# Issuing the output weight's four transfers from SyncE, between two chunks' loads, in a fused retention and gated-unit kernel

## The chip, the cores and the metric

The kernel runs on one core of a Trainium2 chip. A core has five engines that run side by side [...]: TensorE (matrix products, PE in the profile), VectorE (DVE), ScalarE (ACT), GpSimd (POOL) and SyncE (SP), which here does nothing but issue transfers. Each engine takes its instructions in program order, so an instruction that waits holds up all that stand behind it on the same engine. Transfers between HBM and the on-chip memory are issued by SyncE or ScalarE and carried by 16 DMA engines. The metric is the device time of one execution in microseconds (us), median over runs; lower is better.

## The reference

A retention layer (attention without softmax, with an exponential decay per head) feeds a gated linear unit whose gate is a causal convolution. In essence, with B = 8, H = 8 heads, S = 576 positions, D = 64, and a model width of 512:

```python
scores = (q @ k.transpose(0, 1, 3, 2)) / sqrt(D)
Dmat   = where(rel >= 0, gamma[h] ** rel, 0)         # rel = i - j
x      = ((scores * Dmat) @ v)                       # heads side by side: (B, S, 512)
gate   = sigmoid(sum_k conv_w[k] * x[:, s - 4 + k])  # five causal taps per channel
out    = (gate * (x @ w_val)) @ w_out
```

All inputs and the output are float32. `w_val` and `w_out` are 512 x 512 (1 MB each); q, k and v have 9.4 MB each.

## The kernel before

The sequence of each batch is cut into two "double chunks" of 256 positions and a tail of 64; the tails of four batches are gathered into one more chunk of the same size. That gives 18 chunks, numbered m = 0 to 17 here (so the fourth and the fifth are m = 3 and m = 4). The whole order of instructions is written out by hand (`manual_schedule`), so what an engine does next is read off the program text.

For each chunk the work goes through these steps.

- **Loads** (`load`, line 98, through `fetch`, line 85): k, q and v of the chunk, 512 KB each, all issued by SyncE (line 90; 95 for the gathered tails). Chunks 0 to 2 have buffers of their own; later ones share two buffers per tensor (`LB = 2`), so chunk m + 2 can be loaded only when chunk m has been cast out of its buffer. Loads up to chunk 4 are issued ahead of the loop (lines 106 to 124); the loop issues chunk m + 4 at the end of iteration m (line 595).
- **Casts** to bf16 (`cast_k`, `cast_q`, `cast_v`, lines 226 to 239), mostly on GpSimd, for chunk m + 2 in iteration m.
- **Turning** keys and queries with TensorE transposes (`turn`, line 253), copied out by ScalarE (`take_turned`, line 262, into the tile `kq`).
- **Scores** (line 277), masked by VectorE (`masks`, line 287, tile `p`), products with v (`values`, line 309), the **state** that carries earlier positions (`update`, line 356, tile `st`; copied out by ScalarE in `take_state`, line 367, as `sd` or `sl`) and its use (`carried`, line 316). VectorE takes the result as `x` (`take_x`, line 335); GpSimd copies its last four positions into the next chunk (`pass_on`, line 347).
- **The gated unit**, one or two chunks behind: the convolution as products with diagonals (`conv`, line 386, tile `dg`), the sigmoid on ScalarE (`gate`, line 401), the product with `w_val` (`value`, line 406; weights `wvb`, cast from `wvf` by `prep_wv`, line 211), and the product with `w_out` (`project`, line 416; weights `wob`), whose result ScalarE copies out (`ob`, line 428) and SyncE stores (line 430).

The loop (line 504) runs iteration m for chunk m. TensorE's order inside one iteration is: first scores, convolution of chunk m - 1, state, second scores, turning of chunk m + 1's keys, part of the gated unit, values, turning of chunk m + 1's queries, the rest of the gated unit. A "stage" below is the time from one iteration's first scores to the next one's.

`w_out` is used for the first time in iteration 3, where `prep_wo` (line 126) casts the two halves of the tile `wof` into `wob`, one on ScalarE, one on VectorE (lines 567 and 568). `wof` is loaded by `load_wo` (line 118): four transfers of 256 KB, each filling 64 partitions of two of the four column blocks, in the order of `ORDER` (line 114). They are issued by ScalarE, and `load_wo` is called in iteration 1, after that iteration's two copies of turned keys and queries (line 562). The next instruction of ScalarE is iteration 2's first `take_state`.

Of the kernel before, what the change touches and what calls it, by code (L numbers as in the profile page):

```python
# [21 lines left out]
def kernel(  # L22
# [10 lines left out]
    nc = tc.nc  # L33
# [4 lines left out]
    HP = 64  # L38
# [42 lines left out]
    with tc.manual_schedule():  # L81
# [16 lines left out]
        def load(name, m):  # L98
            t = ld.tile([P, H, R, D], F32, name=f"f{name}" + ("e" if m < 3 else ""),
                        bufs=3 if m < 3 else LB)  # L100
            fetch(nc.sync, t, {"q": q, "k": k, "v": v}[name], m)
            loaded[name, m] = t
# [12 lines left out]
        wof = consts.tile([P, NP, DM], F32, name="wof")  # L115
        wob = consts.tile([P, NP, DM], BF16, name="wob")

        def load_wo():
            src = moe_w_out.rearrange("(pr ab hl p) n -> ab hl p pr n", pr=2, ab=2, hl=2)
            for (p0, blk, ab, hl) in ORDER:  # L120
                nc.scalar.dma_start(out=wof[p0:p0 + HP, blk:blk + 2, :], in_=src[ab, hl])

        for name in "kqv":
            load(name, 4)

        def prep_wo(copy, part):
            copy(wob[:, 2 * part:2 * part + 2], wof[:, 2 * part:2 * part + 2])  # L127
# [113 lines left out]
        def run(*lists):  # L241

            for k in range(max(map(len, lists), default=0)):
                for group in lists:
                    for f in group[k] if k < len(group) else []:
                        f()
# [30 lines left out]
        def scores(m, r, spare=False):  # L277
            s = [ps_g.tile([P, NP, P], F32, name="g") if spare else ps_s.tile([P, NP, P], F32, name=f"s{i}")
                 for i in range(2)]
            sps[m, r] = s  # L280
            n = P if dcs[m][0] == "full" else TAIL
            return [[mm(s[i][half[ab], pr, 0:n], lhsT=kq[m][half[i], 0, pr, r, half[ab]],
                        rhs=kq[m][half[i], 1, pr, cols(m, r), half[ab]],
                        start=(pr == 0), stop=(pr == NP - 1))
                     for i in range(2) for ab in range(2)] for pr in range(NP)]

        def masks(m, r, i):
            p = pp.tile([P, NP, P], BF16, name=f"p{i}")
            n = P if dcs[m][0] == "full" else TAIL
            nc.vector.tensor_tensor(p[:, :, 0:n], sps[m, r][i][:, :, 0:n],  # L290
                                    mask[dcs[m][0], r].unsqueeze(1).to_broadcast([P, NP, n]), op=ALU.mult)
            pt[m, r, i] = p
# [63 lines left out]
        def update(m, ab):  # L356
            if m >= ND or dcs[m][0] != "full":
                return []
            kind, b, c = dcs[m]
            if b not in st:  # L360
                st[b] = ps_st.tile([P, NP, D], F32, name="st")
            return [[mm(st[b][half[i], pr, :], lhsT=kbf[m][half[ab], pr, r, i, :],
                        rhs=vbf[m][half[ab], head(pr, i), r, :],
                        start=(c == 0 and ab == 0 and pr == 0 and r == 0), stop=(c == NCH - 1 and ab == 1 and r == R - 1))
                     for r in range(R) for i in range(2)] for pr in range(NP)]

        def take_state(m, ab):

            if m >= ND or dcs[m][0] != "full":
                return  # L370
            kind, b, c = dcs[m]
            last = ab == 1 and c == NCH - 1
            t = tp_sb.tile([P, NP, D], BF16, name="sl" if last else "sd", bufs=GB if last else 4)
            nc.scalar.copy(t, st[b])  # L374
            before[("tail", b) if last else (m, 1) if ab == 0 else (m + 1, 0)] = t
# [10 lines left out]
        def conv(n):  # L386

            g = [ps_g.tile([P, 2, 2 * P], F32, name="g") for _ in range(2)][::-1]
            gps[n] = g
            gsb[n] = {}  # L390
            lists = [], []
            for pr in range(2):
                a, b = 2 * pr, 2 * pr + 1
                for kk in range(KC):
                    for bank, rows, blks in ((0, half[1], (a, b)), (1, half[0], (a, b))):
                        lists[bank].append([mm(g[bank][half[i], pr, :], lhsT=dg[rows, blks[i], kk, :],
                                               rhs=xs(n, rows, blks[i], kk), start=(pr == 0 and kk == 0),
                                               stop=(pr == 1 and kk == KC - 1)) for i in range(2)])
            return lists

        def gate(n, i):
            t = gp.tile([P, 2, 2 * P], F32, name=f"gate{i}")
            nc.scalar.activation(t, gps[n][i], AF.Sigmoid)  # L403
            gsb[n][i] = t
# [99 lines left out]
        for m in range(1, ND + 1):  # L504
            now, nxt, last = ok(m), ok(m + 1), m == ND
            late = m < 4
            hi, lo = conv(m - 1)

            if now and m > 1:
                run(scores(m, 0))  # L510
                masks(m, 0, 0)
                masks(m, 0, 1)
            if last:
                run(lo, hi)
                gate(m - 1, 1)
                gate(m - 1, 0)
            elif late:
                run(lo[0:8], hi[0:8])
                run(pairs(update(m, 0)), hi[8:10])
                take_state(m, 0)  # L520
                gate(m - 1, 0)
                run(pairs(update(m, 1)), lo[8:10])
                take_state(m, 1)
                gate(m - 1, 1)
                run(carried(m, 1))
            else:
                run(carried(m, 1))
                run(pairs(update(m, 1)), lo[0:2])
                take_state(m, 1)
                run(lo[2:10], hi[0:8])  # L530
                gate(m - 1, 1)
                run(pairs(update(m + 1, 0)), hi[8:10])
                take_state(m + 1, 0)
                gate(m - 1, 0)
            if now:
                run(scores(m, 1))
                masks(m, 1, 0)
                masks(m, 1, 1)

            if last:  # L540
                value(m - 1, 1, spare(ps_s, "s1"))
                value(m - 1, 0, spare(ps_s, "s0"))
                project(m - 2, 0)
                project(m - 2, 1)
                project(m - 1, 0, last=True)
                project(m - 1, 1, last=True)
                continue
            def turn_keys():
                if nxt:
                    bank = turn(0, m + 1)  # L550
                    take_turned(0, m + 1, bank)

            def turn_queries():
                if nxt:
                    bank = turn(1, m + 1, spare(ps_g, "g", [P, NP, R, P], BF16) if m == 1 else None)
                    take_turned(1, m + 1, bank)

            if m != 2:
                turn_keys()
            if m == 1:  # L560
                turn_queries()
                load_wo()

            if m == 2:
                prep_wv(s_copy, 0)
            if m == 3:
                prep_wo(s_copy, 0)
                prep_wo(v_copy, 1)
            for (f, n, i) in {1: (), 2: ((value, 0, 1), (value, 0, 0)),
                              3: ((value, 2, 1), (project, 0, 0), (project, 0, 1))}.get(  # L570
                                  m, ((value, m - 1, 1), (project, m - 2, 0))):
                f(n, i)
            if m == 2:
                turn_keys()
            if ok(m + 2):
                cast_k(m + 2)
                cast_q(m + 2)
                cast_v(m + 2)

            run(*values(m, 1))  # L580
            run(*values(m, 0))
            run(carried(m, 0))
            take_x(m, 0)
            take_x(m, 1)
            pass_on(m)

            if m > 1:
                turn_queries()
            for (f, n, i) in {1: (), 2: ((value, 1, 1), (value, 1, 0)),
                              3: ((value, 2, 0), (project, 1, 0), (project, 1, 1))}.get(  # L590
                                  m, ((value, m - 1, 0), (project, m - 2, 1))):
                f(n, i)
            for name in "kqv":
                if ok(m + 2 + LB):
                    load(name, m + 2 + LB)
            if m == 3:
                run(update(m + 1, 0))
                take_state(m + 1, 0)
# [28 lines left out]
```

## Time and profile before

| | |
|---|---|
| device time, median of three runs | 176.76 us (175.93 to 177.71) |
| span of the profiled execution | 177.2 us |
| TensorE busy (matmul) | 146.5 us, 83% |
| VectorE busy | 102.9 us, 58% |
| ScalarE busy | 92.8 us, 52% |
| GpSimd busy | 82.2 us, 46% |
| moved by DMA | 40.35 MB, mean 228 GB/s |
| mean granted TensorE clock | 0.949 |

The profile shows the span in 40 slices of 4.43 us, with a digit for the busy tenths of each engine. They tell stages with different limits apart, which the shares above average away:

```profile
PE   7658840069879999999998899999999999999870
ACT  3745610062376657576565557657565765643340
POOL 4898686400803626334764864468456344000000
PEclk9987998556999999999999999999999999999998
DMA  4999999999203695889999998999999686122134
```

Three stretches can be seen: a start in which the loads of the first chunks and the setup of masks and decay factors share the engines; a hole of TensorE and a slow recovery between 25 and 50 us; and a long, even part in which TensorE is nearly always busy and one stage takes about 7.5 us. In the lists of waits a line "A x <- B y" says that engine A, before its instruction that writes x, sat idle until engine B's instruction y ended; the numbers are the total in us, how often, and the longest. PEclk is the clock that TensorE was granted, in tenths of full speed. In timelines the columns are start, duration, engine, line and instruction, with the idle time before it in brackets. "SPq" and "ACTq" are the issue of transfers by SyncE and ScalarE.

### The profile page before, as it was taken

To read this page: it belongs to the slowest core of one execution; us is meant where nothing else is said; L and a number is where in the kernel's file an instruction comes from. 1 tells how busy PE (TensorE), PEld (TensorE's weight loads), DVE (VectorE), ACT (ScalarE), POOL (GpSimd) and SP (SyncE) were. 2 spreads that over 40 slices of the span, in tenths; PEclk is the share of its full clock that TensorE was granted. 3 is DMA by queue.
4 is the path that set the end of the run, shared out by engine and by line. 5 is a ranking of instruction groups with operands and counts; after the bars stand their busy time and mean duration, and the time that the engine had idled before them with its cause. 6 is when DMAs were issued, how large, how long until landed. Compare 5 with 4: busy or idle time off the path is not lost.

```text
span 177.2 us, 7698 instructions
## 1 busy us (share of the span) xinstructions
PE 146.5 (83%) x3348; PEld 107.4 (61%) x3381; DVE 102.9 (58%) x187; ACT 92.8 (52%) x151; POOL 82.2 (46%) x120
## 2 busy tenths in 40 slices
PE   7658840069879999999998899999999999999870
PEld 2235730057655867778676677677678776776620
DVE  6893550025654566777645576677667776766220
ACT  3745610062376657576565557657565765643340
POOL 4898686400803626334764864468456344000000
PEclk9987998556999999999999999999999999999998
DMA  4999999999203695889999998999999686122134
GB/s 141 347 347 367 353 295 283 268 233 269 78 4 118 221 292 159 187 218 292 303 340 304 313 292 256 287 276 302 286 278 289 155 185 223 64 95 82 67 118 118
DMA packets 69631, 40.35 MB, mean 228 GB/s; under 512 B 14794, under 2 KB 63966, under 8 KB 69598
## 3 DMA queue, kind: packets, MB, share of 16 engines
q1 hardware_dynamic: 68832, 38.54, 74.6%
q10 hardware_dynamic: 766, 1.32, 2.9%
q8 instruction: 26, 0.43, 1.0%
q14 instruction: 7, 0.06, 0.1%
HBM read 30.42 MB, written 9.44 MB: 225 GB/s over the span
## 4 chain that ended last, share of the span: by engine, by line
PE 70%; SPq 13%; DMA 6%; ACT 4%; issue 3%; DVE 1%; ACTq 0%
PE g L410 17%; PE g L420 16%; SPq L90 12%; PE g L249 11%; PE tps L259 10%; PE o L304 7%; PE s L249 5%; DMA fv<-in_v_dram 3%; DMA wof<-in_moe_w_out_dram 3%; PE st L249 3%; ACT kq L267 1%; PE s L410 1%; SPq L110 1%; ACT ob L428 1%; ACT sd L374 1%
## 5 line engine op out<-in xcount | busy, mean ns | idle before, releaser
L290 DVE TENSOR_TENSOR p<-s,mask 128x512 bf16<-128x512 f32 x62 | 39.9, 686 | 31.6 <-PE s L249 31.6
L267 ACT COPY kq<-tps 128x1024 bf16<-128x1024 bf16 (+2 forms) x33 | 32.6, 991 | 15.6 <-PE tps L259 15.3
L420 PE MATMUL g<-wob,z 128*128 128x512 bf16 x113 | 34.6, 379 | 2.9 <-ACT wob L127 1.2
L410 PE MATMUL g<-x,wvb 128*128 128x256 bf16 x272 | 36.6, 281 | 0.2 <-ACT gate L403 0.2
L428 ACT COPY ob<-g 128x512 f32<-128x512 f32 x34 | 19.9, 585 | 25.0 <-PE g L420 22.8
L237 POOL TENSOR_TENSOR vb<-fv,gin 128x1024 bf16<-128x1024 f32 x15 | 28.5, 1902 | 8.7 <-DMA fv<-in_v_dram 8.5
L249 PE MATMUL g<-x,dg 64*64 64x256 bf16 x720 | 30.7, 273 | 1.3 <-DVE x L339 0.6
L339 DVE TENSOR_TENSOR x<-o,gout 128x512 bf16<-128x512 f32 x32 | 22.1, 744 | 15.8 <-PE o L304 15.8
L410 PEld LDWEIGHTS <-wvb 128*128 128x128 bf16 x288 | 27.3, 100 | 4.0 <-issue 0.6
L413 DVE TENSOR_TENSOR z<-gate,g 128x512 bf16<-128x512 f32 x34 | 23.4, 687 | 8.9 <-PE g L410 8.1
L403 ACT ACTIVATE gate<-g 128x512 f32<-128x512 f32 x36 | 21.3, 604 | 10.5 <-DVE p L290 5.4
L249 PEld LDWEIGHTS <-dg 64*64 64x64 bf16 x720 | 23.1, 105 | 4.1 <-issue 2.3
L249 PE MATMUL st<-vb,kb 64*64 64x64 bf16 x512 | 13.8, 195 | 13.1 <-ACT sd L374 12.9
L352 POOL COPY x<-x 128x16 bf16<-128x16 bf16 x16 | 3.1, 196 | 45.6 <-DVE x L339 44.4
L223 POOL CAST qb<-fq 128x512 bf16<-128x512 f32 x30 | 17.6, 613 | 10.7 <-DMA fq<-in_q_dram 9.8
L420 PEld LDWEIGHTS <-z 128*128 128x128 bf16 x144 | 14.0, 98 | 11.9 <-issue 1.6
L249 PEld LDWEIGHTS <-kb 64*64 64x64 bf16 x512 | 12.3, 111 | 14.3 <-issue 14.3
L374 ACT CAST sd<-st 128x256 bf16<-128x256 f32 x24 | 8.9, 370 | 21.3 <-DMA wof<-in_moe_w_out_dram 13.6
L223 POOL CAST kb<-fk 128x512 bf16<-128x512 f32 x30 | 17.6, 613 | 5.2 <-DMA fk<-in_k_dram 3.8
L249 PE MATMUL s<-kq 64*64 64x128 bf16 (+1 forms) x560 | 16.6, 220 | 3.2 <-DVE kq L267 1.2
L249 PEld LDWEIGHTS <-kq 64*64 64x64 bf16 x576 | 11.9, 108 | 10.4 <-issue 10.4
L304 PEld LDWEIGHTS <-vb 64*64 64x64 bf16 x576 | 9.0, 112 | 7.7 <-issue 7.6
(74 smaller groups left out, 133.0 us busy)
## 6 DMA issues: line engine op xcount, KB each, us to landing
out_dram<-ob SPq DMA_DIRECT2D x32, 256.0 KB, 3.7
fk<-in_k_dram SPq DMA_DIRECT2D x26, 256.0 KB, 4.6
fq<-in_q_dram SPq DMA_DIRECT2D x26, 256.0 KB, 5.2
fv<-in_v_dram SPq DMA_DIRECT2D x26, 256.0 KB, 5.7
fke<-in_k_dram SPq DMA_DIRECT2D x3, 512.0 KB, 6.0
fqe<-in_q_dram SPq DMA_DIRECT2D x3, 512.0 KB, 5.4
fve<-in_v_dram SPq DMA_DIRECT2D x3, 512.0 KB, 6.0
wvf<-in_moe_w_val_dram SPq DMA_DIRECT2D x1, 1024.0 KB, 8.7
```

What stands on the lines that cost most here:

```text
L223: copy(dst[:, i], src[:, :, 1:3] if i else src[:, :, 0::3])
L237: eng.tensor_tensor(vbf[m][:, h:h + n], loaded["v", m][:, h:h + n], g[:, h:h + n].unsqueeze(3).to_broadcast([P, n, R, D]), op=ALU.mult)
L249: return lambda: nc.tensor.matmul(*a, skip_group_check=True, **kw)
L267: copy(kq[m][:, which, o:o + n], bank[:, o:o + n])
L290: nc.vector.tensor_tensor(p[:, :, 0:n], sps[m, r][i][:, :, 0:n], mask[dcs[m][0], r].unsqueeze(1).to_broadcast([P, NP, n]), op=ALU.mult)
L304: nc.tensor.matmul(o, start=key not in opened, stop=False, skip_group_check=True, **kw)
L339: nc.vector.tensor_tensor(xg[b // GB][c][:, b % GB, :, x0:x0 + P].rearrange("p o (n r) -> p o r n", r=R), ops[m, ab], gout[:, :, t0:t0 + P ...
L403: nc.scalar.activation(t, gps[n][i], AF.Sigmoid)
L410: nc.tensor.matmul(vps[:, j, :], lhsT=wvb[:, o, 2 * i + j, :], rhs=xs(n, slice(0, P), o, PAD), start=(j == 0 and o == 0), stop=(j == 1 and ...
L413: nc.vector.tensor_tensor(z, gsb[n][i], vps, op=ALU.mult)
L420: nc.tensor.matmul(o, lhsT=zsb[n, j // 2][:, j % 2, i * P:(i + 1) * P], rhs=wob[:, j, :], start=(j == 0), stop=(j == NP - 1))
L428: nc.scalar.copy(ob, o)
```

## The change

The four transfers of `w_out` are issued by SyncE in place of ScalarE, and earlier in the program: `load_wo` is now called right where it is defined, after the loads of chunk 3 have been issued and before those of chunk 4. Its call in iteration 1 is gone. Tiles, shapes, the casts of `w_out` and all else stay as they were. It is meant to keep ScalarE free of transfers in the middle of the computation, and to have `w_out` in the same queue as the loads, in an order chosen by hand.

```diff
@@ -118,8 +118,9 @@
         def load_wo():
             src = moe_w_out.rearrange("(pr ab hl p) n -> ab hl p pr n", pr=2, ab=2, hl=2)
             for (p0, blk, ab, hl) in ORDER:
-                nc.scalar.dma_start(out=wof[p0:p0 + HP, blk:blk + 2, :], in_=src[ab, hl])
-
+                nc.sync.dma_start(out=wof[p0:p0 + HP, blk:blk + 2, :], in_=src[ab, hl])
+
+        load_wo()
         for name in "kqv":
             load(name, 4)
 
@@ -559,7 +560,6 @@
                 turn_keys()
             if m == 1:
                 turn_queries()
-                load_wo()
 
             if m == 2:
                 prep_wv(s_copy, 0)
```

## The prediction

> **What bounds the kernel now.** I read the page's list of costliest groups first, then all waits from 18 to 60 us, then ScalarE's timeline, SyncE's and TensorE's over that stretch, then the table by stage. Over the span TensorE is the busiest engine (146.5 of 177.2 us), and from 53.9 us to the end the chain of waits runs almost wholly through it. An average says nothing of one hole, though, and the page's slices show one: TensorE has two slices at 0 (each 4.43 us, from 26.6 us). The waits of that stretch name who is missing:
>
> ```profile
> POOL x L352 <- DVE x L339: 18.7, 2, 11.8
> DVE p L290 <- PE s L249: 18.2, 5, 13.2
> PEld L249 <- issue: 14.7, 7, 11.7
> ACT sd L374 <- DMA wof<-in_moe_w_out_dram: 13.6, 1, 13.6
> PE st L249 <- ACT sd L374: 12.5, 3, 11.6
> ```
>
> Columns: total us, times, longest. Four engines have one wait of 11.6 to 13.6 us each, and they form a chain: GpSimd's copy waits for VectorE's x, VectorE for TensorE's scores, TensorE for ScalarE's copy of the state (sd, line 374), ScalarE for "wof". ScalarE's own timeline shows what that is:
>
> ```profile
> 21.89 1.02 ACT L267 COPY kq<-g 128x1024 bf16<-128x1024 bf16 x1
> 28.94 7.50 ACTq L121 DMA_DIRECT2D wof<-in_moe_w_out_dram  x4
> 36.48 0.37 ACT L374 CAST sd<-st 128x256 bf16<-128x256 f32 x1 [13.57 <-DMA wof<-in_moe_w_out_dram]
> 36.75 0.60 ACT L403 ACTIVATE gate<-g 128x512 f32<-128x512 f32 x1
> ```
>
> Columns: start, duration, instruction, idle before. ScalarE ends a copy at 22.91, the next four instructions in its order are the w_out issues, the first starts at 28.94, the fourth ends at about 36.4, and the sd copy starts at once. That copy does not read w_out; it stands behind the issues. TensorE has been done with its input since 25.27 us:
>
> ```profile
> 25.01 0.26 PE L249 MATMUL st<-vb,kb 64*64 64x64 bf16 x6
> 36.90 0.26 PE L249 MATMUL st<-vb,kb 64*64 64x64 bf16 x3 [11.61 <-ACT sd L374]
> ...
> 38.14 3.59 PE L410 MATMUL g<-x,wvb 128*128 128x256 bf16 x16
> 41.53 1.06 PE L259 MATMUL tps<-ident,kb 128*128 128x128 bf16 x8
> ```
>
> Why do four issues last so long? SyncE's timeline is a row of loads without a pause, and the DMA share is full; the tables (core, stretch, busy times, then PEclk, DMA share, GB/s):
>
> ```profile
> 22.96:25.30 2.34, 1.75 (x68) 1.45 (x68) 2.12 (x4) 0.00 (x0) 1.73 (x4) 1.00 1.02 287
> 25.30:36.90 11.60, 0.00 (x0) 0.00 (x0) 0.00 (x0) 0.42 (x2) 6.22 (x7) 0.68 1.07 271
> 36.90:41.60 4.70, 4.70 (x57) 3.47 (x57) 1.98 (x3) 2.34 (x5) 0.00 (x0) 0.50 1.17 243
> 41.60:46.00 4.40, 4.17 (x69) 3.55 (x67) 2.74 (x4) 2.02 (x2) 1.11 (x3) 0.83 0.99 245
> 46.00:51.00 5.00, 4.04 (x129) 3.27 (x129) 3.50 (x7) 2.74 (x6) 3.17 (x4) 1.00 0.02 6
> ```
>
> From 25.3 to 36.9 TensorE does nothing while the DMA engines are full; from 36.9 to 41.6 it works at half clock; from 46 on the DMA is empty, because everything that the two load buffers hold has landed. So ScalarE pays, by standing still, for bytes that nobody needs before 50.6 us (VectorE's half of the wob cast).
>
> [...]
>
> **The change, part by part.** I count chunks from 0, so the fourth and fifth are 3 and 4.
>
> *Removed from ScalarE:* four issues and the wait around them. The sd copy can start when TensorE's input is ready, at 25.27 us. The previous chunk shows the pattern: state matmuls to 19.15, sd at 19.18, the next state matmuls at 19.60. So TensorE resumes at about 25.7 in place of 36.9: 11.2 us.
>
> *Clock:* without the hole TensorE stays at the 1.00 it has at 22.96 to 25.30. I rebuild chunk 2 from durations seen at full clock. After 25.7, the rest of the state, carried and score matmuls take 0.7 us (chunk 1: 19.60 to 20.32), so to 26.4; eight value matmuls 0.87 (the chain of waits, any later chunk) to 27.3. The next eight need the wvb cast that ScalarE does after sd, gate, sd, gate: from 36.48 to 39.52 that sequence takes 3.0 us; started at 25.3 it ends about 28.2. So 28.2 + 0.87 = 29.1. Key transposes 0.55: 29.6. ScalarE's kq copy 1.0: 30.7. Query transposes 0.6: 31.3. Sixteen value matmuls 1.76: 33.0. Chunk 3's scores, at 46.0 before, so start at 33.0. The saving is 13.0 us: 11.2 of the hole and 1.8 of clock (sixteen value matmuls alone took 3.52 us at half clock against 1.76).
>
> *Added to SyncE:* four issues of 256 KB between chunk 3's last load (issued to about 21.5) and chunk 4's first (21.53). [...] Behind them stand the loads of chunks 4, 5, 6. The price is DMA time for 1.05 MB. Between 20 and 45 us queue q1 moved 5.81 MB in 91.9% of 25 us (253 GB/s) and ScalarE's q10 1.05 MB in 17.4% (241 GB/s): 4.1 to 4.4 us; at the 353 GB/s of an early slice it is 3.0. Only the lower half of the partitions is written by one transfer, the upper by the next; the trace shows no such transfer alone, so as an upper bound I take half the 291 GB/s that q1 averages: 7.2 us. I take 4.1.
>
> *Who waits for that:* chunk 4. Now its k lands at 26.7, q at 29.6, v at 31.1 (issue plus time to landing). With 4.1 more: 30.8, 33.7, 35.2. GpSimd's casts of 1.2, 1.2 and 1.9 us then end at 32.0, 34.9 and 37.1. TensorE turns chunk 4's keys 3.3 us into chunk 3's stage (49.3 against 46.0), so at 36.3; its queries 8.5 us in, at 41.5; its v is needed by the state update at 11.7 us in, 44.7. Slack 4.3, 6.6 and 7.6 us. Even the upper bound of 7.2 leaves about 1 us for the keys. Hidden.
>
> *Chunks 5 and 6:* the total of bytes up to chunk 6 is unchanged; their landing, now up to 40.0 and 46.7, stays there, while TensorE is 13 us earlier. Chunk 5's keys are turned 2.7 us into chunk 4's stage, at 47.5; chunk 6's about 8 us later. Both come in time. The outputs of chunk 3's stage queue behind chunk 6's loads on SyncE (five output buffers for four stores), so no engine waits. The DMA pause at 46 to 53 us, bought by the hole, is eaten up. Later stages are set by TensorE (7.5 us a stage, 7.38 busy), and each load is issued after the stores of its stage as before, so they move as a block.
>
> *w_out itself* lands near 31 us; its casts come about 37.6. No new wait. The 1.2 us that TensorE waits for ScalarE's wob cast stays.
>
> Sum: 176.76 - 11.2 - 1.8 = 163.8 us.
>
> **Rivals.**
> *Only the hole goes.* TensorE's pauses near 23 to 28 us let the clock drop, or the drained DMA costs as much as the clock returns: 176.76 - 11.2 = 165.6. For it: the clock also read 0.83 between 13 and 21 us with work running. Against: 1.00 from 18 us on at a busy share of 0.75.
> *Late data.* SyncE's extra megabyte and chunk 4's loads drain so slowly, or the missing DMA pause shows in chunks 5 to 7, that TensorE waits 3 to 5 us: 167 to 169. For it: DMA share 0.84 and 255 GB/s in the stage from 57.74 us, with GpSimd waiting up to 2.5 us for loads later. Against: the slacks above, and those waits of GpSimd don't enter the chain.
> *The wait only changes its name.* The page's chain goes through v's landing at 31.1 and SyncE's issues, so perhaps chunk 2 waits for loads and not for ScalarE; then 4.1 us more on SyncE is lost time: 176.76 + 4.1, about 181. Against: chunk 2's casts were over by 19.3 us, and TensorE's releaser at 36.9 is sd, which starts as the fourth issue ends.
>
> **How the numbers follow.** The forecast, within 1 us of 163.8: 0.65. Only the hole: 0.17. Late data: 0.08. Renamed: 0.04. A little more gained, near 162 (chunk 3's waits shrink too): 0.06. The range 162.3 to 166.8 takes in the hole alone with an error of about a microsecond and leaves out the late data and the renamed wait. Faster by over 1%: all but the last rival and a tail, 0.95; within 1% 0.02; slower 0.03.
>
> **What would show it.** Right: ScalarE's sd near 25.3 with no long wait; TensorE's clock 1.00 from 25 to 45; no zero slices; chunk 3's scores near 33; the wait of 13.6 us gone, with SyncE issuing wof at 21 to 26 us; kb of chunk 4 cast by about 32. Wrong: TensorE waiting for keys of chunk 4 or a vb cast with GpSimd waiting on a DMA; ScalarE still idle for over 5 us; a stage after chunk 4 longer than 7.5 us by more than a few tenths.

## The result, and the profile after

| | before | after |
|---|---|---|
| device time, median of four runs | 176.63 us (175.93 to 177.71) | 166.36 us (165.41 to 172.81) |
| ratio to before, 95% interval | | 0.940 (0.931 to 0.948) |
| profiled execution: its time, its span | 178.96, 177.2 us | 165.41, 163.7 us |
| TensorE busy, and its share of the span | 146.5 us, 83% | 145.8 us, 89% |

The run at 172.81 us stands apart from the other three and is not part of the ratio. The ratio is a saving of 10.7 us (9.2 to 12.2) on 176.63. TensorE does the same work in both; what went is its idle time. The changed file is one line longer at that place, so line 249 of before is 250 here, 374 is 375, and so on.

The longest waits between 18 and 60 us of the changed kernel (total, times, longest), to be read against the five of before:

```profile
DVE p L291 <- PE s L250: 10.1, 7, 3.5
POOL x L353 <- DVE x L340: 7.4, 2, 4.7
ACT sd L375 <- PE st L250: 6.1, 3, 3.8
PEld L250 <- issue: 5.4, 10, 0.9
```

No wait is as long as 5 us, wof is no releaser any more, and the direction has turned: ScalarE's sd now waits for TensorE (3.8 us at most), not TensorE for sd. ScalarE's timeline of the changed kernel has nothing between its last kq copy and sd:

```profile
21.10 1.05 ACT L268 COPY kq<-g 128x1024 bf16<-128x1024 bf16 x1
25.97 0.37 ACT L375 CAST sd<-st 128x256 bf16<-128x256 f32 x1 [3.81 <-PE st L250]
```

TensorE's timeline at the same place:

```profile
23.10 0.52 PE L250 MATMUL g<-x,dg 64*64 64x256 bf16 x10 [0.48 <-DVE x L340]
24.28 1.37 PE L250 MATMUL g<-x,dg 64*64 64x256 bf16 x22 [0.66 <-issue]
...
26.39 0.26 PE L250 MATMUL st<-vb,kb 64*64 64x64 bf16 x3 [0.32 <-ACT sd L375]
...
34.00 0.42 PE L250 MATMUL s<-kq 64*64 64x128 bf16 x16
```

The wait ahead of the state matmuls has shrunk from 11.61 to 0.32 us. Chunk 3's first scores start at 34.00 in place of 46.02. A pause of 0.66 us stands in the convolution, which the profile of before in the prediction did not have. The table by stage of the changed kernel (core, stretch, busy times, PEclk, DMA share, GB/s) shows where the clock went:

```profile
21.00:25.00 4.00, 2.32 (x81) 1.69 (x84) 2.54 (x4) 1.15 (x2) 3.41 (x6) 0.93 1.06 306
25.00:29.00 4.00, 3.46 (x82) 2.58 (x70) 1.26 (x2) 2.75 (x6) 2.08 (x3) 0.64 1.09 270
29.00:33.00 4.00, 3.46 (x68) 3.12 (x69) 2.79 (x5) 1.66 (x3) 1.39 (x3) 1.00 1.16 326
```

Even without the hole the clock fell for some microseconds (0.64 from 25 to 29, 1.00 again from 29 on), but not for the 10 us and more of before (0.50 in the whole of 30 to 42). And the transfers went where they were meant to, in SyncE's timeline:

```profile
21.54 3.08 SPq L121 DMA_DIRECT2D wof<-in_moe_w_out_dram  x4
24.67 1.15 SPq L90 DMA_DIRECT2D fk<-in_k_dram  x2
```

Chunk 4's first load is issued at 24.67, 3.1 us later than before (21.53). The next sections ask whether that costs anything, and what exactly made ScalarE stand still.

### The profile page after: what moved, and what is told of

Its sections match the earlier page's. It is cut to its first block, busy times and chain, and to the rows that moved or that the text cites. A ratio compares the mean times of both kernels' runs of the same rounds, so it can differ in the third digit from the quotient of the medians.

```text
span 163.7 us, 7699 instructions
## 1 busy us (share of the span) xinstructions
PE 145.8 (89%) x3348; PEld 106.7 (65%) x3381; DVE 102.8 (63%) x187; ACT 92.5 (56%) x151; POOL 82.8 (51%) x120
## 4 chain that ended last, share of the span: by engine, by line
PE 79%; ACT 6%; DVE 5%; issue 4%; DMA 2%; ACTq 0%
PE g L421 18%; PE g L411 17%; PE g L250 14%; PE tps L260 11%; PE o L305 8%; PE s L250 6%; PE st L250 4%; DMA fke<-in_k_dram 2%; DVE dg L209 2%; ACT kq L268 2%; PE s L411 1%; ACT sd L375 1%; ACT ob L429 1%; DVE kb L224 1%; DVE p L291 1%
## 5 line engine op out<-in xcount | busy, mean ns | idle before, releaser
L411 PE MATMUL g<-x,wvb 128*128 128x256 bf16 x272 | 35.2, 273 | 0.6 <-ACT wvb L215 0.3
L250 PE MATMUL g<-x,dg 64*64 64x256 bf16 x720 | 31.8, 277 | 2.6 <-issue 1.1
L340 DVE TENSOR_TENSOR x<-o,gout 128x512 bf16<-128x512 f32 x32 | 22.1, 744 | 13.9 <-PE o L305 13.9
L411 PEld LDWEIGHTS <-wvb 128*128 128x128 bf16 x288 | 26.6, 98 | 3.9 <-ACT wvb L215 0.6
L375 ACT CAST sd<-st 128x256 bf16<-128x256 f32 x24 | 8.9, 370 | 10.7 <-PE st L250 7.4
L305 PEld LDWEIGHTS <-vb 64*64 64x64 bf16 x576 | 8.4, 107 | 7.6 <-issue 7.4
```

What stands on the lines that cost most here:

```text
L250: return lambda: nc.tensor.matmul(*a, skip_group_check=True, **kw)
L305: nc.tensor.matmul(o, start=key not in opened, stop=False, skip_group_check=True, **kw)
L340: nc.vector.tensor_tensor(xg[b // GB][c][:, b % GB, :, x0:x0 + P].rearrange("p o (n r) -> p o r n", r=R), ops[m, ab], gout[:, :, t0:t0 + P ...
L411: nc.tensor.matmul(vps[:, j, :], lhsT=wvb[:, o, 2 * i + j, :], rhs=xs(n, slice(0, P), o, PAD), start=(j == 0 and o == 0), stop=(j == 1 and ...
```

## The experiments

The theory: an issue by ScalarE has to wait its turn while SyncE's loads fill the transfer path, whatever its own size, and ScalarE's next work waits behind it. Its rivals: w_out's own megabyte has to drain; or the early place in SyncE's queue is what helps. All times below have a ratio to the kernel before, timed on the same chip in the same session, with its 95% interval. "Chunk 2's stage" is the time from chunk 2's first scores to chunk 3's on TensorE: 23.06 us in the profile of before (22.96 to 46.02), 11.80 after (22.20 to 34.00).

**Before and after once more.** The kernel before was profiled two more times, unchanged.

> The kernel before once more, for a second profile. If the hole of ScalarE is a property of the program, the wait ahead of the sd copy is 12 to 14 us again and TensorE has two empty slices; the length of the half-clock stretch behind it may differ by some us.

> The kernel before once more, for a third profile: the stage of chunk 2 was 23.06 and 22.47 us in the two profiles there are, and what came after chunk 3's scores 131.2 and 135.1 us. If the typical execution is nearer to 176 us, the stage should be again 22 to 23 us, and the rest near 130 to 132.

Chunk 2's stage was 22.47 (22.13 to 44.60) and 22.32 us (22.11 to 44.43), with TensorE's wait for sd at 9.35 and 10.31 us, in executions of 181.37 and 179.44 us. What comes after chunk 3's scores was 135.1 and 133.3 us, longer than I expected; in both the clock fell a second time for some microseconds (mean 0.89 from 120 to 135 us in the first, 0.89 from 90 to 105 in the second), far from the change. The slices of the first of them:

```profile
PEclk9999965559999999999999999999699999999997
```

The 6 and 5s at slices 6 to 9 are the hole, the single 6 at slice 29 is that later fall. It comes and goes: executions of the variants below have it too (0.89 from 105 to 120 us with GpSimd's cast, 0.93 from 120 to 135 with the two dummy matmuls), while the changed kernel's profile reads 1.00 from 60 to 160. Both new profiles of before also have the pause of some 0.65 us in chunk 2's convolution, so it does not come with the change. Together with the first profile, all three profiled executions of before (178.96, 181.37, 179.44 us) lie near or above the upper end of the unprofiled ones (174.97 to 179.37 in 27 runs).

> The changed kernel once more, timed for a tight interval. My step of 13.0 us (11.2 hole, 1.8 clock) gives a ratio of 0.926; the hole alone 0.937. A ratio near 0.94 would say that the clock term was too large for the typical run.

Ratio 0.942 (0.933 to 0.951), median 166.31 us. Chunk 2's stage in this profile was 10.53 us (22.65 to 33.18), with the clock at 1.00 throughout and no such pause in the convolution.

**The same four transfers by SyncE, from the old place.**

```diff
-                nc.scalar.dma_start(out=wof[p0:p0 + HP, blk:blk + 2, :], in_=src[ab, hl])
+                nc.sync.dma_start(out=wof[p0:p0 + HP, blk:blk + 2, :], in_=src[ab, hl])
 ...
                 turn_queries()
                 load_wo()        # stays here
```

> The four transfers issued by SyncE, but from the old place in the program (iteration 1, so behind chunk 4's loads and ahead of chunk 5's). Theory (the issuing engine is what counts, not the place in the queue): within 1 us of the changed kernel, about 165 to 167 us, chunk 4 landing about 4 us earlier than in it. Rival (the early place is what counts): a good part of the 11 us comes back, above 170 us.

Ratio 0.939 (0.930 to 0.949), chunk 2's stage 11.74 us (22.18 to 33.92). The move within the program gives nothing that these runs can tell (the interval is about 1.7 us to either side); the engine is what counts. GpSimd's cast of chunk 4's keys started at 27.35 us in place of 31.23, and nobody used the gain.

**Four tiny issues by ScalarE.** On top of the changed kernel:

```diff
+        tiny = consts.tile([HP, 4, 4], F32, name="tiny")
+        def load_tiny():
+            for t in range(4):
+                nc.scalar.dma_start(out=tiny[:, t, :], in_=moe_w_out[0:HP, 4 * t:4 * t + 4])
 ...
                 turn_queries()
+                load_tiny()
```

> The changed kernel, and in addition four tiny transfers (16 bytes on each of 64 partitions, 1 KB each, of which nothing is used) issued by ScalarE at the old place. Theory (ScalarE's issue waits its turn behind SyncE's loads in a full transfer path, whatever its own size): ScalarE stands still for 8 to 13 us again and the time is 173 to 178 us. Rival (w_out's own megabyte has to drain before ScalarE is free): four issues of about 0.6 us each, sd at most 1 to 3 us late, 165 to 168 us.

Ratio 1.003 (0.998 to 1.007): four transfers of 1 KB give back the whole gain. ScalarE's timeline of this run:

```profile
21.88 1.05 ACT L274 COPY kq<-g 128x1024 bf16<-128x1024 bf16 x1
28.15 6.27 ACTq L127 DMA_DIRECT2D tiny<-in_moe_w_out_dram  x4
34.46 0.37 ACT L381 CAST sd<-st 128x256 bf16<-128x256 f32 x1 [11.53 <-DMA tiny<-in_moe_w_out_dram]
```

It is the picture of before with other bytes: 5.2 us until the first issue, 6.3 for four, of which each is recorded as about half a microsecond (median 479 ns), so most of the time lies before and between them. The size of what ScalarE transfers is no cause. TensorE waits 7.36 us for sd here, and the clock falls as before (0.50 from 26 to 38 us).

**One tiny issue.** The same with `range(1)`.

> The changed kernel with one tiny transfer (1 KB, unused) issued by ScalarE at the old place, in place of four. Theory (each ScalarE issue waits its own turn behind SyncE's issues): the first of four started about 6 us after ScalarE was free, so sd comes at about 28.5 instead of 25.4 and the time is 3 to 5 us above the changed kernel, 169 to 171 us. Rival (the wait is one wait for the transfer path to empty, however many issues): as with four, about 177 us.

Median 172.09 us, ratio 0.973 (0.957 to 0.989): between the two, so the cost grows with the number of issues. The time is 1 us above the upper end of my estimate. ScalarE's and TensorE's timelines:

```profile
28.50 0.54 ACTq L127 DMA_DIRECT2D tiny<-in_moe_w_out_dram  x1
29.08 0.37 ACT L381 CAST sd<-st 128x256 bf16<-128x256 f32 x1 [6.10 <-DMA fv<-in_v_dram]
```

```profile
25.93 1.49 PE L256 MATMUL g<-x,dg 64*64 64x256 bf16 x22 [1.50 <-issue]
...
29.50 0.26 PE L256 MATMUL st<-vb,kb 64*64 64x64 bf16 x3 [1.66 <-ACT sd L381]
```

sd came when expected, but the clock fell once more (0.50 from 26 to 34 us), and the work from TensorE's restart to chunk 3's scores took 9.13 us (29.50 to 38.63) against 7.61 after. That is what I left out. Note the releaser: the profile names v's landing, though sd does not read v. It is the issue in front of sd that waited for v.

**What an issue of ScalarE waits for.** The chain of waits (start, duration, what) names it. First the end of the hole with four tiny issues, then the step with one, then a step in the kernel before:

```profile
26.85 7.08 DMA wof<-in_moe_w_out_dram
33.95 0.47 ACTq L127
34.42 0.04 issue
34.46 0.38 ACT sd L381
```

```profile
21.31 7.16 DMA fv<-in_v_dram
28.50 0.54 ACTq L127
```

```profile
25.36 5.73 DMA fv<-in_v_dram
31.09 0.02 issue
31.11 5.35 DMA wof<-in_moe_w_out_dram
```

Each time a transfer of SyncE lands, and ScalarE's issue starts at once. In the trace's records every one of these issues carries a wait for a semaphore. In the traces of before and after, the 157 transfers of SyncE and ScalarE report their landings on eight semaphores in all, which the two engines share. The first issue on each carries no wait, the other 149 do, and ScalarE's four of the kernel before started when the transfer before them on the same semaphore had landed. Nothing in the kernel's text says so.

The four tiny issues start at 28.15, 30.85, 31.94 and 33.95 us; the landings on their semaphores, one of v and three of w_out, all issued by SyncE, came at 28.13, 30.83, 31.92 and 33.92. In the kernel before, the four issues wait in turn for a load of q (landed 28.92, issue 28.94), one of v (31.09, 31.11), one of k (33.11, 33.13), and the last for w_out's own first transfer (35.81, 35.83). Of the 21 such issues by ScalarE in six profiles, 20 start 0.02 to 0.03 us after that landing; the other stands behind the issue in front of it. So the issue does not stand in front of a full path, as my theory has it: the shared semaphore makes ScalarE wait for a landing, and behind the other loads a landing of 256 KB comes late (6.1 to 7.2 us after its issue here; the first 512 KB of the program landed in 3.9).

**ScalarE issues at the start of the program.** The kernel before with `load_wo()` called ahead of the loop, still on ScalarE.

```diff
+        load_wo()
         for name in "kqv":
             load(name, 4)
 ...
                 turn_queries()
-                load_wo()
```

> The kernel before, but ScalarE issues its four w_out transfers at the start of the program, right after the small convolution weight. Theory (what hurts is a ScalarE issue while SyncE's loads fill the path and other engines need ScalarE): no hole at 25 us; the start is later by the 3 to 4 us of transfer that w_out puts among chunk 0's and 1's loads, and ScalarE's exponentials by some us; 168 to 171 us. Rival (any issue by ScalarE costs the same): about 177 us.

Median 169.84 us, ratio 0.962 (0.949 to 0.976), as expected. ScalarE's four issues, and what TensorE pays:

```profile
1.47 2.79 ACTq L121 DMA_DIRECT2D wof<-in_moe_w_out_dram  x4
```

```profile
14.35 0.44 PE L250 MATMUL st<-vb,kb 64*64 64x64 bf16 x16 [3.59 <-POOL vb L238]
```

Four issues take 2.79 us here, against 13.5 us with the wait ahead of them in the middle of the loads: three use semaphores that no transfer has used yet, the fourth one whose transfer landed at 2.92, before the issue at 3.64. Chunk 2's stage is 10.20 us (26.74 to 36.94), so the hole is gone; the price is chunk 0's v, behind a megabyte that nobody needs yet. Early is not good in itself: in the changed kernel the megabyte stands behind everything that is urgent.

**More bytes in front of chunk 4.** The changed kernel with another 0.75 MB behind w_out.

```diff
         load_wo()
+        more = consts.tile([P, 3, DM], F32, name="more")
+        for j in range(3):
+            nc.sync.dma_start(out=more[:, j, :], in_=moe_w_out[j * P:(j + 1) * P, :])
```

> The changed kernel with another 0.75 MB (three transfers of 256 KB of w_out's rows into a tile that nobody reads) behind w_out on SyncE, so chunk 4 comes about 3 us later still. Theory (chunk 4 has over 4 us of slack before TensorE needs its keys): within 1 us of the changed kernel. Rival (chunk 4's lateness is on the path): 3 us slower, about 169 us.

Ratio 0.940 (0.925 to 0.954), median 166.61 us: the same as the changed kernel. GpSimd's cast of chunk 4's keys, and TensorE's turning of them:

```profile
34.03 1.17 POOL L227 CAST kb<-fk 128x512 bf16<-128x512 f32 x2 [5.99 <-PE tps L263]
```

```profile
38.92 0.62 PE L263 MATMUL tps<-ident,kb 128*128 128x128 bf16 x8
```

The cast ends at 35.2, 3.7 us ahead of its use, even with 1.8 MB in front of the loads (in this profile TensorE turns them some 1.6 us later than in the changed kernel's: its chunk 2 starts 0.7 us later, and the clock reads 0.50 from 26 to 30 us, where that one's reads 0.77). The bracket names TensorE, but the later half of k landed at 33.88, just ahead of the cast. Chunk 4's lateness is hidden.

**The clock by itself.** The kernel before, with TensorE kept busy in the hole.

```diff
                 run(pairs(update(m, 0)), hi[8:10])
+                if m == 2:
+                    keep_warm(45, spare(ps_t, "tps"))
                 take_state(m, 0)
```

> The kernel before, with 45 dummy matmuls of 512 columns (about 9.7 us at full clock, written to a free bank, not used) put on TensorE where it stands in the hole. ScalarE's wait stays, so the hole stays; only the clock is kept up. My clock term says 1.8 us faster than before, ratio 0.99, granted clock 1.00 from 37 to 45 us and the sixteen value matmuls at 1.8 in place of 3.5 us. If the clock is no part of it: the ratio is 1.00 and the stage from the hole's end to chunk 3's scores stays at 9.1 us.

Ratio 0.9945 (0.991 to 0.998): 1.0 us of 175.7 (0.3 to 1.6). TensorE's timeline:

```profile
25.14 9.66 PE L445 MATMUL tps<-zeros 128*128 128x512 bf16 x44 [0.16 <-issue]
35.71 0.22 PE L249 MATMUL st<-vb,kb 64*64 64x64 bf16 x3 [0.92 <-ACT sd L374]
...
43.12 0.42 PE L249 MATMUL s<-kq 64*64 64x128 bf16 x16
```

With TensorE busy in the hole the clock read 1.00 from 22 to 50 us, where the first profile of before has 0.93 from 26 to 30, 0.50 from 30 to 42 and 0.87 from 42 to 46. From restart to chunk 3's scores it is 7.41 us, against 9.12, 9.12 and 8.87 in the profiles of before (36.90 to 46.02, 35.48 to 44.60, 35.56 to 44.43). The clock is part of the gain, about 1.5 to 1.7 us in profiled executions and 1.0 in timed ones.

**Keeping the clock up in the changed kernel** (`keep_warm(2, spare(ps_t, "tps"))` ahead of chunk 2's scores).

> The changed kernel with two dummy matmuls of 512 columns ahead of chunk 2's scores, where TensorE pauses for ScalarE's copy. Theory (the pauses near 22 to 24 us sometimes drop the clock, which cost 1.0 us in one profile of the changed kernel and nothing in another): clock 1.00 from 22 to 30 us and the stage of chunk 2 at 10.1 to 10.6 us; median 0 to 1 us below the changed kernel. If two matmuls are too few: the clock still drops to about 0.8 there, the time is the changed kernel's.

Ratio 0.942 (0.935 to 0.949): nothing gained. The clock stayed at 1.00 from 22 to 30 us, but a pause of 0.99 us stood in the convolution and the stage took 11.32 us (22.03 to 33.35), over my range.

**A version that uses w_out's early landing.** With w_out on chip by 30.0 us in the profile of the changed kernel, its cast can leave ScalarE in iteration 3, where TensorE waits for it; the changed kernel's line:

```profile
39.99 1.89 PE L421 MATMUL g<-wob,z 128*128 128x512 bf16 x7 [1.23 <-ACT wob L128]
```

First only ScalarE's half was moved, then both.

```diff
-            if m == 3:
-                prep_wo(s_copy, 0)
-                prep_wo(v_copy, 1)
+            if m == 2:
+                prep_wo(g_copy, 0)
 ...
                 f(n, i)
+            if m == 2:                   # the second version; in the first
+                prep_wo(v_copy, 1)       # VectorE's half stayed in m == 3
```

> The changed kernel, with the half of the w_out cast that ScalarE does in iteration 3 given to GpSimd in iteration 2, ahead of chunk 4's casts: possible since w_out now lands near 30 us. It takes away the 1.2 us that TensorE waits for wob. If that wait is on the path: 1.2 us faster than the changed kernel, about 165 us, and no wait of TensorE for wob. If GpSimd's later casts of chunk 4 then hold up the keys: no gain or slower.

> The changed kernel with both halves of the w_out cast moved to iteration 2: ScalarE's half to GpSimd ahead of chunk 4's casts, VectorE's half to the end of VectorE's work of iteration 2. TensorE should wait for no half of wob: chunk 3's stage (scores to scores) about 1.2 us shorter than the changed kernel's, 165 us, a ratio to the kernel before near 0.93. If VectorE's 0.7 us then delays chunk 3's masks on the path: half of that gain is lost.

The first gave 0.937 (0.924 to 0.950), which can't be told from the changed kernel; a wait of 0.58 us for VectorE's half took the place of part of the one removed. The second gave 0.926 (0.918 to 0.934), median 163.96 us; on the same chip the kernel with the two dummy matmuls, equal to the changed one in its ratio, had 166.25. Its two lines on TensorE show no wait between the products:

```profile
37.38 1.04 PE L411 MATMUL g<-x,wvb 128*128 128x256 bf16 x8
38.26 2.04 PE L421 MATMUL g<-wob,z 128*128 128x512 bf16 x7
```

Chunk 3's stage is 10.67 us (33.65 to 44.32) where it was 11.91 both before (46.02 to 57.93) and after (34.00 to 45.91): 1.24 us, the wait that was removed. The medians differ by 2.3 us; the rest of that is not explained. This version has the lowest ratio of all, though its interval overlaps those of the changed kernel itself (0.931 to 0.948 and 0.933 to 0.951), which was timed in other sessions.

## Why the prediction was right, and where it was off

*The hole and its cause:* right. sd came at 25.34 and 25.97 us in the two profiles of the changed kernel (25.3 was forecast), and the tiny issues show that the wait belongs to ScalarE's issues and not to the size of what they move. What an issue waits for the prediction did not name: it pointed to the full DMA and read the 13.6 us as the time that four issues last. Each issue was recorded at 0.60 to 0.72 us; the rest was the wait for the landing on its semaphore.

*The place in SyncE's queue:* right that it costs nothing. The last of w_out's four transfers landed at 30.00 us, 4.4 us after the load in front of the first (25.56), where 4.1 was taken; the upper bound of 7.2, my estimate from half of q1's 291 GB/s, was not reached. Chunk 4's keys were cast from 31.23 on (30.8 was forecast for their landing) and turned at 37.27; 0.75 MB more did not show. That the place brings nothing either is shown by the transfers from the old place.

*The size:* the saving was 10.7 us (9.2 to 12.2), not 13.0; the time lies in the range, 2.6 us above the likeliest. Three terms were off.

- The hole, 11.2 us, was taken as the whole distance from 25.7 to 36.9. From chunk 2's first scores to TensorE's restart before took 13.9, 13.4 and 13.5 us in three profiles; after, 4.2 and 3.1, where I had 2.7. The difference of the means is 9.9 us. Part of it is that TensorE came to the state matmuls later: the pause in the convolution and the clock fall, which the first rival named, took 1.0 us in one profile of the changed kernel and were absent in the other.
- The clock, 1.8 us: restart to chunk 3's scores took 7.61 and 7.41 us after (7.3 was forecast) against 8.9 to 9.1, so about 1.5 us in profiles and 1.0 (0.3 to 1.6) in the timed test. With 9.9 that is 11.4 us, inside the interval of the timed saving.
- The base. I subtracted from the median of 176.76 a saving read in an execution that took 178.96. Between the two profiled executions, 178.96 and 165.41, the difference is 13.55 us, near my sum; between the medians it is 10.3.

*The rivals:* "only the hole goes", at 165.6, came nearest. Pauses (0.48 and 0.66 us) and a fall of the clock (0.64 from 25 to 29) stand together in one of the two profiles of the changed kernel; that the one makes the other is not shown, since with the two dummy matmuls a pause of 0.99 us left the clock at 1.00. In part its nearness is luck: it sets the clock's gain at nothing, where 1.0 to 1.7 us was measured, and the hole at 11.2, where it was 9.9. "Late data" and "the wait only changes its name" are excluded, the one by the time that the keys still had in hand with the added bytes, the other by sd's start. The last one's observation was sound, though: the chain goes through v's landing at 31.09 because ScalarE's second issue, at 31.11, waited for it.

*Open:* what the pause of 0 to 1.5 us in chunk 2's convolution waits for (the profile says "issue", that is, nothing it can show); why the later fall of the clock comes in some executions; why the profiled executions of before were long ones; and whether ScalarE's issues in the middle of the loads would be free of the wait if they had a semaphore of their own. None was tried apart.

## What to carry to other kernels

An issue of a transfer is an instruction in its engine's order, and it can wait for the landing of a transfer of another engine: in the kernel before, ScalarE's first issue started at 28.94 us, 0.02 us after a load of SyncE had landed, and sd, whose input was ready at 25.27, started at 36.48, behind the fourth. While another engine's loads run one behind the other, put no issue, however small, on an engine that others wait for (four of 1 KB: ratio 1.003; one: 0.973); give it to the engine that does nothing else, behind what is urgent and ahead of its own use (0.940 here, against 0.962 from ScalarE at the start of the program). Where a wait is named after a transfer that the waiting instruction does not read, look for an issue in front of it. When a saving is read out of one profile, look first at how the time of that execution stands to the median, and read the same distance in a second profile.

## What the runs showed of the hardware

I had not expected size to be so irrelevant. While the loads ran, the issue of a 1 KB transfer by ScalarE started 5.2 and 5.5 us after ScalarE was free, and four of them held it for 11.5 us, for the landings of SyncE's transfers of 256 KB that took 6.1 to 7.2 us from their issue. At the start of the program four of 256 KB were issued in 2.79 us. In the kernel before, w_out's four issues by ScalarE were recorded at 0.60 to 0.72 us each, and their transfers landed 6.9 to 8.2 us after their issue. The long part is the wait in front of an issue: the first started 6.03 us after ScalarE was free (22.91 to 28.94), 0.02 us after the landing on its semaphore.
